# The last sum of each weight conversion job on POOL in place of DVE, in a fused attention, feed-forward and gated-attention kernel

## The chip, the cores and the metric

The kernel runs on one core of a Trainium2 chip. The metric is device time in microseconds of one launch; smaller is better. The engines are named as the profile names them: PE (TensorE), DVE (VectorE), ACT (ScalarE), POOL (GpSimd) and SP, which here only issues transfers.

## The reference

Three blocks follow one another on 4 x 576 tokens of 512 features; the conversion that the change touches prepares weights of the second.

```python
# 1: causal attention, 4 batches, 8 heads, 576 positions, head width 64, bias from cumulative sums
scores = scale * (q @ k.T); cum = cumsum(maximum(s, 0))
scores = where(causal, -1e9, scores + minimum(-(cum_i - cum_j), 0))
x = softmax(scores) @ v
# 2: mixing over positions (U 576x32, V 32x576), feed-forward (512 to 2048 to 512), residual
u = x + (x.T @ U @ V).T
x = u + maximum(u @ w_ch1, 0) @ w_ch2
# 3: four gated causal attention heads, the best two of four per token
out = sum over the chosen e of gate_e * softmax(scale * q_e @ k_e.T) @ v_e @ wo_e
```

`U`, `V`, `w_ch1` and `w_ch2` come to the kernel as bits of float64 (each value two 32-bit words) and have to be made into float32 on the chip.

## The kernel before, in words

**Split operands.** Matmuls of the feed-forward run on operands that are split in a high and a low part: ACT makes the high half as a rounded copy, DVE or POOL the low half as the difference. For weights these are `wh` (L200, ACT) and `wl` (L203, POOL), for the input `uh` (L279, ACT) and `ul` (L280; of four pieces per chunk of 288 tokens three, and in part of the kernel all but one, on POOL).

**Three parts.** Attention (to about 320 us): 32 heads, each in five row blocks, make 160 steps of one loop (`Attn.run`) and ten more to drain it. In a step PE computes a block of scores (`qk`, L364 and L365), DVE adds the mask and takes the row peak (`peak`, L375), ACT does the exponential of the step before (`exp`, L382), PE transposes what is ten steps old (L405, L408), ACT or DVE moves it out of PSUM (L78, L80), and PE multiplies it with the values (L433). When the step number divided by five leaves 1, `norm` divides the head that is done by its row sums: two small DVE operations (L387, L388) and five on POOL (L393). Then `fillers` puts background work into the step: operands of the next heads (L492, L495, L593), pieces of the weight conversion, the mixing, and the first three hidden blocks of the feed-forward.

The feed-forward part (about 320 to 675 us) runs over the other 13 hidden blocks of 128 in groups of 2, 3, 3, 3 and 2, each group over eight chunks of 288 tokens (the first group's last two chunks take the three blocks of attention along). Each step is `ffn1` (12 matmuls, L830; ACT makes `hh`, L834, and DVE its low half `hl`, L835) and, two blocks later, `ffn2` (12 matmuls, L848). At the end of a chunk's group DVE adds four accumulators to the result (L855). While a group is computed, the weights of the next are converted. In the first group the mixing of the last batch runs too (L239 to L265). The last part, the gated attention, has no conversion.

**The conversion.** `f32_stages` makes one job of a piece of weights, mostly 128x256. Its pieces: a load by SP into one of two buffers `c_raw`; a square on ACT (`p0`, L108); a masked multiply on DVE that writes `c_h` (`p1`, L111); then shift (`v0`, L115), sign (`v1`, L120), exponent (`v2`, L124), the low word scaled (`v3`, L129, again into `c_h`) and the sum (`v4`, L133), all on DVE; then `use`: for most weights `wh` on ACT (`v5`) and `wl` on POOL (`v6`). `c_a`, which the sum reads and writes, has two buffers; `c_mk`, `c_h` and `c_z` have one. In attention these three lie in unused columns of the tiles `pt`, and the profile names them so. For the first feed-forward group (`wf`) the sum writes the weights' place itself, and `v5` and `v6` do nothing.

**What sets the order.** The program is put on each engine's queue in the order in which it is written. `f32_stream` interleaves the pieces of neighbouring jobs by a table. In attention it is `STREAM`, in the feed-forward part `PLAIN`; a pair (0, 4) is `v4` of this job, (1, -1) `p1` of the next, (2, -3) the load of the one after:

```python
CONVS = ((1, 1, 1, 1, 1), (2, 2, 2, 2, 2))
PLAIN = (((0, 0),), ((0, 1),), ((0, 2), (1, -2)), ((0, 3),), ((0, 4), (2, -3)), ((1, -1),), ((0, 5),), ((0, 6),))
STREAM = (((0, 0),), ((-1, 5),), ((0, 1),), ((0, 2), (1, -2)), ((-1, 6),), ((0, 3),), ((0, 4), (2, -3)), ((1, -1),))
FAST = (40, 70)
```

In attention, from step 4, one entry of the table is put out per step, and two in steps 41 to 69, after `peak`, `exp` and `norm` of that step; the first and the third entry of the stream are put out ahead of the loop. There are 23 jobs in attention (one for U, two for V, twenty for five hidden blocks) and 12, 12, 12 and 8 in the first four feed-forward groups, where a loop puts out about five entries behind each hidden block from the fourth on (three in the fourth group), after the pieces of the input split.

Of the kernel before, what the change touches and what calls it, by code (L numbers as in the profile page):

```python
# [8 lines left out]
F32 = mybir.dt.float32  # L9
# [78 lines left out]
def f32_stages(nc, pool, width, load, m, n, name, use=None, dest=None, fixed={}):  # L88

    t_ = {}

    def tile_(tag, dt, bufs=1):
        if tag in fixed:
            t_[tag] = fixed[tag][:m, :n].bitcast(dt)
            return t_[tag]
        t_[tag] = pool.tile([P, width], dt, tag=tag, name=f"{tag}_{name}", bufs=bufs)[:m, :n]
        return t_[tag]

    def s0():
        raw = pool.tile([P, width], I64, tag="c_raw", name=f"c_raw_{name}", bufs=2)[:m, :n]
        load(raw)
        words = raw.bitcast(U32).rearrange("p (n w) -> p n w", w=2)
        t_["low"], t_["high"] = words[:, :, 0], words[:, :, 1].bitcast(F32)

    def p0():
        nc.scalar.activation(out=tile_("c_mk", F32), in_=t_["high"], func=AF.Square)  # L108

    def p1():  # L110
        nc.vector.scalar_tensor_tensor(out=tile_("c_h", F32), in0=t_["c_mk"], scalar=TINY * TINY,  # L111
                                       in1=t_["high"], op0=OP.is_ge, op1=OP.mult)

    def v0():
        nc.vector.tensor_scalar(out=tile_("c_a", U32, 2), in0=t_["c_h"].bitcast(U32), scalar1=3, scalar2=0x3FFFFFF8,  # L115
                                op0=OP.logical_shift_left, op1=OP.bitwise_and)

    def v1():

        nc.vector.scalar_tensor_tensor(out=t_["c_a"], in0=t_["c_h"].bitcast(U32), scalar=0xC0000000, in1=t_["c_a"],  # L120
                                       op0=OP.bitwise_and, op1=OP.bitwise_or)

    def v2():
        nc.vector.tensor_scalar(out=tile_("c_z", U32), in0=t_["c_a"], scalar1=0xFF800000, scalar2=None,  # L124
                                op0=OP.bitwise_and)

    def v3():

        nc.vector.scalar_tensor_tensor(out=t_["c_h"], in0=t_["low"], scalar=2.0 ** -52, in1=t_["c_z"].bitcast(F32),  # L129
                                       op0=OP.mult, op1=OP.mult)  # L130

    def v4():
        nc.vector.tensor_tensor(out=t_["c_a"].bitcast(F32) if use else dest(), in0=t_["c_h"],  # L133
                                in1=t_["c_a"].bitcast(F32), op=OP.add)

    def v5():
        if use:
            t_["u"] = use(t_["c_a"].bitcast(F32))
            next(t_["u"])

    def v6():
        if use:
            next(t_["u"], None)

    return [s0, p0, p1, (v0, v1, v2, v3, v4, v5, v6)]


# [1044 lines left out]
```

## Time and profile before

| | |
|---|---|
| time, median of 3 runs | 894.37 us (889.55 to 895.36) |
| profiled execution | 890.45 us, its span 888.6 us |
| granted TensorE clock, mean | 0.983 |
| busy: PE, DVE, ACT, POOL | 831.1, 605.1, 473.5, 308.0 us |
| sums L133 on DVE | 67 |

The span is from the first to the last instruction of the profiled execution; that execution's own time holds 1.85 us more around it. Times in the timelines count from the start of the span. In the rows, "x5" means that so many neighbouring instructions of one line are drawn together, the shape then being that of the first; a value in square brackets is the time that the engine stood idle before, and what it was released by.

### The profile page before, as it was taken

What the parts mean: (1) busy time and instruction counts of PE and PEld (TensorE: products, weight loads), DVE (VectorE), ACT (ScalarE), POOL (GpSimd) and SP (SyncE); (2) the same over time, 40 slices, a digit from 0 to 9 for tenths busy, and PEclk for the clock granted to TensorE, in tenths of its full rate; (3) what the DMA queues carried; (4) which work ended last, traced back from release to release, by engine and by line L of the source; (5) the groups of instructions that cost most, each with busy time, mean ns of one, the idle gap of its engine ahead of it and who ended that gap; (6) DMA issues with size and microseconds to landing.
All of it is one profiled execution on the core that took longest, in us unless ns stands there. A gap on an engine that the chain in (4) does not pass through costs nothing.

```text
span 888.6 us, 17507 instructions
## 1 busy us (share of the span) xinstructions
PE 831.1 (94%) x6008; PEld 745.7 (84%) x6008; DVE 605.1 (68%) x1763; ACT 473.5 (53%) x1406; POOL 308.0 (35%) x458
## 2 busy tenths in 40 slices
PE   3787988899998989999999999999999999999997
PEld 2565766688886879899999999999999999888875
DVE  7688888687577529986885788577446676646541
ACT  6577768767567353333442443333333467565673
POOL 4435454344433333322342342233233033221241
PEclk9799899899999999999999999999999999999999
DMA  8877578676662051221111121111000121211221
GB/s 217 198 200 202 148 180 214 156 184 184 182 163 69 27 192 43 49 58 27 49 49 48 48 61 48 49 44 53 1 2 1 33 49 29 63 45 35 61 68 54
DMA packets 36944, 79.65 MB, mean 90 GB/s; under 512 B 4792, under 2 KB 7992, under 8 KB 36856
## 3 DMA queue, kind: packets, MB, share of 16 engines
q1 hardware_dynamic: 36856, 78.53, 33.6%
q8 instruction: 48, 0.79, 0.4%
q14 instruction: 40, 0.33, 0.1%
HBM read 38.80 MB, written 8.40 MB: 53 GB/s over the span
## 4 chain that ended last, share of the span: by engine, by line
PE 75%; DVE 9%; DMA 5%; ACT 4%; issue 3%; POOL 2%; SPq 1%; DVEq 0%; ACTq 0%; POOLq 0%
PE hps L830 17%; PE facc L848 17%; PE pv L433 7%; PE qkp L1039 6%; PE t L405 5%; PE qk L364 4%; PE vps L976 3%; PE ops L1062 3%; PE qk L365 3%; DMA c_raw_w<-in_w_dram 3%; PE hps L296 3%; PE facc L310 3%; PE t L408 2%; ACT P L382 1%; PE mt L251 1%
## 5 line engine op out<-in xcount | busy, mean ns | idle before, releaser
L280 POOL TENSOR_TENSOR ul<-uT,uh 128x288 fp32r<-128x288 f32 x126 | 103.5, 839 | 176.7 <-ACT uh L279 164.6
L375 DVE CUSTOM_DVE_ANT_0 P<-qk,mask 64x64 f32<-64x64 f32 (+4 forms) x240 | 116.8, 488 | 61.0 <-PE qk L365 36.8
L382 ACT ACTIVATE P<-P,stat 64x64 f32<-64x64 f32 (+4 forms) x240 | 133.6, 557 | 39.7 <-DVE stat L375 37.5
L393 POOL TENSOR_SCALAR P<-P,stat 64x64 f32<-64x64 f32 (+4 forms) x160 | 101.6, 649 | 142.4 <-DVE stat L388 93.8
L364 PE MATMUL qk<-R,L 128*128 128x288 f32 (+4 forms) x288 | 98.5, 347 | 24.2 <-DVE L L577 9.8
L834 ACT ACTIVATE hh<-hps 128x288 fp32r<-128x288 f32 x110 | 44.8, 407 | 135.0 <-PE hps L830 134.6
L848 PE MATMUL facc<-hh,wh 128*128 128x288 f32 x376 | 111.2, 296 | 0.5 <-DVE aT L855 0.5
L830 PE MATMUL hps<-ul,wh 128*128 128x288 f32 x376 | 111.2, 296 | 0.0
L830 PE MATMUL hps<-uh,wl 128*128 128x288 f32 x376 | 111.1, 296 | 0.0
L830 PE MATMUL hps<-uh,wh 128*128 128x288 f32 x376 | 111.0, 295 | 0.0
L848 PE MATMUL facc<-hh,wl 128*128 128x288 f32 x376 | 110.9, 295 | 0.0
L848 PE MATMUL facc<-hl,wh 128*128 128x288 f32 x376 | 110.8, 295 | 0.0
L78 ACT ACTIVATE pt<-t 64x64 f32<-64x64 f32 (+5 forms) x304 | 90.4, 336 | 36.9 <-PE t L408 28.3
L835 DVE SCALAR_TENSOR_TENSOR hl<-hps,hh 128x288 fp32r<-128x288 f32 x110 | 50.1, 456 | 87.6 <-ACT hh L834 87.3
L405 PE MATMUL t<-ident,P 128*128 128x128 f32 x480 | 91.2, 289 | 11.0 <-issue 4.1
L393 POOL TENSOR_SCALAR P<-P,stat,pt 64x64 f32<-64x64 f32 (+4 forms) x80 | 48.2, 615 | 127.5 <-DVE stat L388 50.7
L433 PE MATMUL pv<-pt,V 128*64 128x320 f32 (+4 forms) x672 | 85.3, 378 | 7.3 <-ACT uT L78 7.3
L364 PEld LDWEIGHTS qk<-R,L 128*128 128x128 f32 x288 | 58.0, 202 | 38.9 <-issue 20.1
L365 PE MATMUL qk<-R,L 68*128 68x288 f32 (+9 forms) x288 | 90.1, 318 | 0.3
L405 PEld LDWEIGHTS t<-ident,P 128*128 128x128 f32 x480 | 60.2, 145 | 23.4 <-issue 14.0
L433 PEld LDWEIGHTS pv<-pt,V 128*64 128x64 f32 x672 | 43.7, 140 | 40.9 <-issue 12.4
L203 POOL TENSOR_TENSOR wl<-c_a_w,wh 128x256 fp32r<-128x256 f32 x56 | 43.3, 773 | 93.6 <-ACT wh L200 86.1
(177 smaller groups left out, 2211.5 us busy)
## 6 DMA issues: line engine op xcount, KB each, us to landing
c_raw_w<-in_w_dram SPq DMA_DIRECT2D x64, 256.0 KB
uT<-in_qk_dram SPq DMA_DIRECT2D x15, 576.0 KB
L<-HI SPq DMA_DIRECT2D x28, 288.0 KB
R<-HI SPq DMA_DIRECT2D x28, 288.0 KB
V<-in_v_dram SPq DMA_DIRECT2D x16, 320.0 KB
R<-uT SPq DMA_DIRECT2D x14, 288.0 KB
L<-uT SPq DMA_DIRECT2D x14, 288.0 KB
aD<-stage SPq DMA_DIRECT2D x6, 576.0 KB
```

The source lines that it names most:

```text
L78: nc.scalar.activation(out=out, in_=in_, func=AF.Copy)
L280: eng.tensor_tensor(out=l_, in0=src, in1=h_.bitcast(F32), op=OP.subtract)
L364: nc.tensor.matmul(ps[:, bk, :w], lhsT=q1[:, rows], rhs=k1[:, c0:c0 + w], start=True, stop=False)
L365: nc.tensor.matmul(ps[:, bk, :w], lhsT=q2[:, rows], rhs=k2[:, c0:c0 + w], start=False, stop=True)
L375: nc.vector.tensor_tensor_reduce(out=po, in0=view, in1=mk, scale=-1.0, scalar=3.0e38, op0=OP.add, op1=OP.min, accum_out=stat[P - M:, 0, t: ...
L382: nc.scalar.activation(out=po, in_=po, func=AF.Exp, scale=-1.0, bias=stat[P - M:, 0, t:t + 1], accum_out=stat[P - M:, 1, t:t + 1])
L393: nc.gpsimd.tensor_scalar(out=pv, in0=pv, scalar1=stat[r0:, 2, t:t + 1], scalar2=1.0 if gate is None else gate(t)[r0:], op0=OP.mult, op1=O ...
L405: nc.tensor.transpose(ps[:, P * kb:P * kb + P], Pn[:, c0:c0 + P], ident)
L433: nc.tensor.matmul(ps[64 * hh:64 * hh + 64, lo - a:e - a], lhsT=V(hh)[:, kb, :], rhs=pt[:, PST * kb + lo:PST * kb + e], start=kb == 0, sto ...
L830: nc.tensor.matmul(ps, lhsT=w[:, 0, cs], rhs=x, start=i == 0, stop=i == 11)
L848: nc.tensor.matmul(accs[c][d], lhsT=w[:, 1, cs], rhs=x, start=f == fs[0] and i == 0, stop=f == fs[-1] and i == 2)
L1039: nc.tensor.matmul(ps[:, :HALF], lhsT=wsl(w, "qk", k, col, col + P), rhs=xx[:, c0:c0 + HALF], start=i == 0, stop=i == 11)
```

## The change

The sum `v4` is issued on POOL instead of DVE. Operands, sizes and its place in the written order stay the same, and so does all else.

```diff
     def v4():
-        nc.vector.tensor_tensor(out=t_["c_a"].bitcast(F32) if use else dest(), in0=t_["c_h"],
+        nc.gpsimd.tensor_tensor(out=t_["c_a"].bitcast(F32) if use else dest(), in0=t_["c_h"],
                                 in1=t_["c_a"].bitcast(F32), op=OP.add)
```

## Rows read from the trace of the kernel before

**Rows 1.** The page of the profile: busy time of each engine; the chain by engine.

```profile
PE 831.1 (94%) x6008; PEld 745.7 (84%) x6008; DVE 605.1 (68%) x1763; ACT 473.5 (53%) x1406; POOL 308.0 (35%) x458
...
PE 75%; DVE 9%; DMA 5%; ACT 4%; issue 3%; POOL 2%; SPq 1%; DVEq 0%; ACTq 0%; POOLq 0%
```

**Rows 2.** Busy us by stretch (instructions in brackets), then PE clock, DMA share, GB/s.

```profile
60.00:100.00 40.00, 32.09 (x218) 24.41 (x215) 32.03 (x107) 30.81 (x100) 18.33 (x28) 0.92 0.80 205
...
343.00:403.00 60.00, 57.37 (x422) 56.19 (x421) 53.82 (x124) 20.09 (x55) 19.08 (x23) 1.00 0.19 49
```

**Rows 3.** What PE waited for, 345 to 403 us: total us, times, longest.

```profile
PE facc L848 <- DVE aT L855: 1.7, 2, 1.2
PE hps L830 <- DVE hl L835: 0.7, 1, 0.7
```

**Rows 4.** Timeline of PE, 357 to 371 us: start, us, operation [idle before].

```profile
357.43 0.40 PE L830 MATMUL hps<-uh,L 128*128 128x288 f32 x1 [0.69 <-DVE hl L835]
...
370.06 0.40 PE L848 MATMUL facc<-hh,L 128*128 128x288 f32 x1 [1.16 <-DVE aT L855]
```

**Rows 5.** What DVE waited for, 403 to 470 us, then 547 to 625 us.

```profile
DVE hl L835 <- ACT hh L834: 12.8, 14, 2.7
...
DVE hl L835 <- ACT hh L834: 23.9, 23, 2.7
```

**Rows 6.** Instructions of lines L133 and L203: ns minimum/median/maximum, first and last start.

```profile
L133 DVE TENSOR_TENSOR c_a_w<-c_h_w,c_a_w x44: 408/424/1060, 342.6 to 630.5; 128x256 f32<-128x256 f32 x44
L133 DVE TENSOR_TENSOR c_a_w<-pt,c_a_w x12: 415/425/548, 63.0 to 166.6; 128x256 f32<-128x256 f32 x12
...
L203 POOL TENSOR_TENSOR wl<-c_a_w,wh x56: 722/739/1230, 68.0 to 631.4; 128x256 fp32r<-128x256 f32 x56
```

**Rows 7.** Timeline of DVE in attention, around three of the jobs.

```profile
49.59 0.42 DVE L133 TENSOR_TENSOR c_a_v<-pt,c_a_v 128x288 f32<-128x288 f32 x1
...
50.94 0.56 DVE L111 SCALAR_TENSOR_TENSOR pt<-pt,c_raw_w 128x256 f32<-128x256 f32 x1
...
109.62 0.19 DVE L388 RECIPROCAL stat<-stat 128x5 f32<-128x5 f32 x1
...
112.72 0.42 DVE L111 SCALAR_TENSOR_TENSOR pt<-pt,c_raw_w 128x256 f32<-128x256 f32 x1
...
261.52 0.42 DVE L133 TENSOR_TENSOR wf<-pt,c_a_w 128x256 f32<-128x256 f32 x1
...
264.23 0.42 DVE L111 SCALAR_TENSOR_TENSOR pt<-pt,c_raw_w 128x256 f32<-128x256 f32 x1
```

**Rows 8.** Timeline of POOL around the same three jobs.

```profile
49.87 2.98 POOL L393 TENSOR_SCALAR P<-P,stat 64x64 f32<-64x64 f32 x5 [5.03 <-PE t L408]
...
110.00 4.31 POOL L393 TENSOR_SCALAR P<-P,stat 64x64 f32<-64x64 f32 x5 [2.58 <-PE mo L262]
...
261.08 4.10 POOL L393 TENSOR_SCALAR P<-P,stat 64x64 f32<-64x64 f32 x5 [5.88 <-DVE stat L388]
```

**Rows 9.** Timeline of DVE in the feed-forward part.

```profile
341.14 0.92 DVE L124 TENSOR_SCALAR c_z_w<-c_a_w 128x256 uint32<-128x256 uint32 x1
...
342.56 0.42 DVE L133 TENSOR_TENSOR c_a_w<-c_h_w,c_a_w 128x256 f32<-128x256 f32 x1
343.07 0.43 DVE L111 SCALAR_TENSOR_TENSOR c_h_w<-c_mk_w,c_raw_w 128x256 f32<-128x256 f32 x1
...
347.11 0.29 DVE L124 TENSOR_SCALAR c_z_w<-c_a_w 128x256 uint32<-128x256 uint32 x1
...
383.28 0.91 DVE L133 TENSOR_TENSOR c_a_w<-c_h_w,c_a_w 128x256 f32<-128x256 f32 x1
384.23 0.92 DVE L111 SCALAR_TENSOR_TENSOR c_h_w<-c_mk_w,c_raw_w 128x256 f32<-128x256 f32 x1
```

**Rows 10.** Timeline of POOL in the feed-forward part.

```profile
339.36 2.55 POOL L280 TENSOR_TENSOR ul<-uT,uh 128x288 fp32r<-128x288 f32 x3 [6.71 <-ACT uh L279]
...
382.16 2.70 POOL L280 TENSOR_TENSOR ul<-uT,uh 128x288 fp32r<-128x288 f32 x3 [2.71 <-ACT uh L279]
```

## The prediction

> **What bounds the kernel now.** I read the page first, for the shares of the engines and of the chain that ended last, then the busy time by stretch, then who waited for whom, and last the rows of DVE and POOL one by one around each conversion.
>
> The page says that TensorE carries 75% of the chain and DVE 9%; POOL is busy 35% of the span against DVE's 68% [rows 1]. The stretches say where it could count. In attention (up to about 320 us) no engine is full: from 60 to 100 us PE is busy 32.1 of 40 us and DVE 32.0 [rows 2], and the steps hand work round between PE, DVE, ACT and POOL. In the feed-forward part only 343 to 403 us is different: DVE is busy 53.8 of 60 us and PE has 2.6 us without work [rows 2]. All that its waits put down to an engine is DVE: 1.7 us for the sums that empty the accumulators (L855) and 0.7 us for the low halves (L835), two of them at 357 and 370 us [rows 3, 4]. In the three groups behind it PE never waits, and DVE has 12.8 us (first) to 23.9 us (last of the three) in which it waits for ACT [rows 5]. The last conversion sum starts at 630.5 us [rows 6]; behind it nothing is changed.
>
> **What the change removes.** There are 67 conversion jobs: 23 in attention, 44 in the feed-forward part. Each loses one DVE sum of about 0.42 us [rows 6]: 23 x 0.42 = 9.7 us of DVE in attention, 44 x 0.42 = 18.5 us behind it.
>
> **What it adds.** The same sum on POOL. The nearest row is L203, also a two-input fp32 operation over 128x256, at 0.74 us [rows 6]; I take that. The hand-over to POOL shows where the normalisation follows the reciprocal: that ends at 109.81 and POOL starts at 110.00, 0.19 us [rows 7, 8]. For the way back I allow 0.1 us, an estimate; 0 and 0.2 are its bounds.
>
> It also adds a wait. The next job's masked multiply (L111) overwrites c_h, of which there is one buffer, and the sum reads c_h. While both were on DVE the order cost nothing. Now L111 waits for POOL, and behind it in DVE's queue stand the row peaks (L375), the low halves and the accumulator sums, for which ACT and PE wait. In front of the sum in POOL's queue stand normalisations (five operations, 3 to 4.3 us) and u splits (L280). The raw loads on SP depend on v3, not on the sum, so they move only as DVE moves; the copy wh (L200) comes behind L111 in both orders and wl (L203) behind wh.
>
> **Attention.** A job's sum and the next L111 lie one step of the loop apart. From the written order of pieces the sum of job k falls on step 10, 18, 26, 34, then every fourth from 41 to 69, then every eighth from 77 to 157. Where the step number leaves 1 or 2 on division by five, a normalisation has just been put ahead of it in POOL's queue. That holds for nine jobs; in two of them (57 and 157) POOL is idle again or nothing follows, so seven wait. The first: the sum was ready at 49.59, POOL normalises until 52.85, so the sum ends at 53.6 and L111, which ran at 50.94, can start at 53.7: 2.75 us later [rows 7, 8]. One in the middle: 114.31 + 0.84 = 115.15 against 112.72, 2.43 us. The last: 265.18 + 0.84 = 266.02 against 264.23, 1.79 us [rows 7, 8]. The seven are 2.75, 2.23, 2.43, 1.87, 2.23, 0.99 and 1.79: 14.3 us. Each DVE sum that is gone gives 0.42 back, so DVE runs 14.3 - 2.9 = 11.4 us late in all, 1.6 us at each of seven places.
>
> How much reaches the end? At least nothing, at most 11.4. A case comes about every 40 us, and DVE idles 8 us in a stretch of that length [rows 2], five times the delay; but that idle time lies between steps that PE feeds, and PE stands as often. I take a quarter, +3.0 us, nearer the lower end.
>
> The other 16 jobs give DVE 16 x 0.42 = 6.7 us. On the chain this is worth DVE's share of 9%, 0.6 us, and at most all 6.7. Against it stands a second effect: the new POOL operation lies over DVE operations. While POOL ran three u splits (339.36 to 341.91), DVE's L124 took 0.92 us; with POOL idle it took 0.29 [rows 9, 10]. One such meeting costs more than the sum gave. I set gain and loss here to nothing, with -6.7 and 16 x 0.63 = +10.1 as ends.
>
> The Trainium skill ("SBUF — State Buffer", section "Who interferes with whom") says that a DVE instruction with two SBUF inputs, or in a two-port mode, and a GpSimd instruction that reads SBUF exclude each other for a whole instruction. The pair of L124 rows agrees. By that rule the 16 free jobs are no gain but a loss wherever such a DVE instruction follows; the end above is that case.
>
> **Feed-forward part.** About five or six pieces are issued one after another per hidden block, so L111 mostly follows the sum at once: 342.56, then 343.07 [rows 9]. With POOL free L111 would start 0.19 + 0.74 + 0.1 = 1.03 us after v3's end instead of 0.51: 0.5 us later per job. Of the twelve jobs between 343 and 404 us nine are adjacent like this. Four of them lie between 350 and 370 us, where DVE never rests more than 0.3 us and PE waits for it: 4 x 0.5, less 0.4 us of DVE idle time, is +1.6. One more, at 383.28, finds POOL in three u splits until 384.86 [rows 9, 10], so L111 moves from 384.23 to 385.7, and the accumulator sums behind it by 1.5 us; I pass on +0.9. Sum +2.5. The ends: all nine passed on and that queue, 9 x 0.5 + 1.5 = 6.0 and, for the three jobs that are not adjacent, 3 x 0.5, +7.5; or the 2.4 us of PE's waits given back, -2.4. In the other 32 jobs 0.5 us each stands against 12.8 us of idle time or more per group [rows 5]: nothing.
>
> **Sum.** +3.0 + 2.5 = +5.5 us. The profiled execution took 890.45 us (span 888.6), so 895.95; the median of the three runs is 894.37, 3.9 above it, which makes 899.9 by the median. I forecast that.
>
> **Rivals.** (a) The waits pass on in full: +11.4 in attention and +7.5 behind, 18.9 in all, 913.3. For it: DVE and PE are both at four fifths in attention, so a late peak is a late PE. Against: DVE's idle time behind each case.
> (b) The port decides: the 16 meetings at 0.63 us cost 10.1 on top of 5.5, +15.6 or 910.0. For it: L124's two rows. Against: many DVE operations beside the sums read PSUM, and one that waits on L111 meets nobody. The Trainium skill's rule ("SBUF — State Buffer", section "Who interferes with whom") leads here if it is carried through all 16.
> (c) All is hidden: 894.4. For it: PE's 75% of the chain. Against: DVE already holds PE up at 357 and 370 us [rows 4].
> (d) Faster: DVE is what attention and the stretch from 343 us wait for, and POOL delivers in time; -6.7 - 2.4 = -9.1, 885.3. It decides from the point at which L111 lies over 1.03 us behind the sum, which most attention jobs without a normalisation ahead fulfil. Against: in the crowded stretch, the one where PE demonstrably waits for DVE, L111 follows at 0.5 us.
>
> **How the numbers follow.** About 1% (8.9 us) is what a measurement of this kernel can tell from no change. The forecast has 0.42, of which 0.05 lies beyond +8.9; (a) 0.22, (b) 0.08, (c) 0.16, (d) 0.12, of which 0.10 beyond -8.9 or so. Slower: 0.05 + 0.22 + 0.08 = 0.35; faster 0.10; within 1%: 0.37 + 0.16 + 0.02 = 0.55. The range leaves out the end of (a) and most of (d): 890 to 911. The forecast's own is 896 to 905.
>
> **What would show it.** Right: L133 appears on POOL 67 times at about 0.74 us; L111 shows idle time before it put down to POOL, 1.0 to 2.8 us at seven places in attention and 0.5 us in the blocks; DVE's busy time falls by about 28 us; PE's waits for L855 and L835 between 343 and 404 us grow from 2.4 to about 5 us; attention ends 2 to 4 us later. Wrong: if attention ends earlier, (d) holds; if L111 doesn't wait but DVE's own operations beside the sums grow to 0.9 us, (b); if attention ends over 8 us later, the waits pass on whole and (a) holds.

## The result and the profile after

The changed kernel takes 897.95 us (median of 11 runs, 895.53 to 901.68) against 892.76 us of the kernel before measured beside it (median of 11, 888.9 to 895.81). The ratio is 1.0065, 95% interval 1.0045 to 1.0084: slower by 5.8 us, 4.0 to 7.5. The forecast was +5.5 us, a factor of 1.0062. The two profiled executions differ as much: spans of 894.5 and 888.6 us.

From the page of the changed kernel, the busy time of each engine and the chain by engine, to be read beside [rows 1]:

```profile
PE 833.9 (93%) x6008; PEld 745.6 (83%) x6008; DVE 577.4 (65%) x1696; ACT 473.5 (53%) x1406; POOL 354.0 (40%) x525
...
PE 74%; DVE 6%; DMA 6%; issue 5%; POOL 4%; ACT 3%; SPq 1%; POOLq 0%; ACTq 0%; DVEq 0%
```

67 instructions left DVE and 67 came to POOL. DVE is busy 27.7 us less, POOL 46.0 us more, and the kernel is slower: DVE's busy time was not what the end waited for.

The sum's line in the changed kernel (ns minimum/median/maximum, first and last start), and below it who waited for it (total us, times), to be read beside [rows 6]:

```profile
L133 POOL TENSOR_TENSOR c_a_w<-c_h_w,c_a_w x44: 727/737/743, 348.4 to 636.2; 128x256 f32<-128x256 f32 x44
L133 POOL TENSOR_TENSOR c_a_w<-pt,c_a_w x12: 727/732/742, 64.8 to 168.4; 128x256 f32<-128x256 f32 x12
...
  ACT wh L200: 64.5, 35
  DVE c_h_w L111: 27.1, 33
  DVE pt L111: 10.7, 8
```

The price of 0.74 us was right. L111 now waits for POOL 41 times: 8 times in attention (its c_h lies in a `pt` tile there), 10.7 us together, and 33 times in the feed-forward part, 27.1 us.

Where the time went is read from two fixed points, first in the kernel before, then in the changed one. The accumulator sums of the feed-forward part that write `aT` (first and last start), in the kernel before:

```profile
L855 DVE TENSOR_TENSOR aT<-facc,aT x128: 441/448/451, 335.2 to 638.0; 128x288 f32<-128x288 f32 x128
```

and in the changed kernel:

```profile
L855 DVE TENSOR_TENSOR aT<-facc,aT x128: 440/447/451, 340.9 to 644.1; 128x288 f32<-128x288 f32 x128
```

The first comes 5.7 us later and the last 6.1 us. By this pair of profiles 5.7 us were lost in attention, and 0.4 us in the stretch in which 44 of the 67 sums run.

In attention, the reciprocal of a head (L388) serves as a milestone. Three of the 32 from the timeline of DVE before (start, us):

```profile
49.49 0.19 DVE L388 RECIPROCAL stat<-stat 128x5 f32<-128x5 f32 x1
...
64.67 0.19 DVE L388 RECIPROCAL stat<-stat 128x5 f32<-128x5 f32 x1
...
299.37 0.19 DVE L388 RECIPROCAL stat<-stat 128x5 f32<-128x5 f32 x1
```

In the changed kernel these three start at 49.06, 66.88 and 305.19 us: 0.4 us early at the first, 2.2 late two heads on, 5.8 late at the end. What lies between the first two is the first of the seven places. DVE there in the changed kernel (in brackets the idle time before and what ended it):

```profile
52.91 0.43 DVE L111 SCALAR_TENSOR_TENSOR pt<-pt,c_raw_w 128x256 f32<-128x256 f32 x1 [2.65 <-POOL c_a_v L133]
...
116.12 0.43 DVE L111 SCALAR_TENSOR_TENSOR pt<-pt,c_raw_w 128x256 f32<-128x256 f32 x1 [1.35 <-POOL c_a_w L133]
...
270.09 0.43 DVE L111 SCALAR_TENSOR_TENSOR pt<-pt,c_raw_w 128x256 f32<-128x256 f32 x1 [0.63 <-POOL wf L133]
```

POOL at the first and the second of these:

```profile
49.44 2.67 POOL L393 TENSOR_SCALAR P<-P,stat 64x64 f32<-64x64 f32 x5 [5.58 <-DVE stat L388]
52.08 0.80 POOL L133 TENSOR_TENSOR c_a_v<-pt,c_a_v 128x288 f32<-128x288 f32 x1
...
111.59 3.79 POOL L393 TENSOR_SCALAR P<-P,stat 64x64 f32<-64x64 f32 x5 [3.97 <-DVE stat L388]
115.36 0.73 POOL L133 TENSOR_TENSOR c_a_w<-pt,c_a_w 128x256 f32<-128x256 f32 x1
```

and ACT behind the first:

```profile
53.92 0.67 ACT L382 ACTIVATE P<-P,stat 128x448 f32<-128x448 f32 x1 [2.60 <-DVE stat L375]
```

This is the chain of the prediction, link by link: the sum starts where the normalisation ends, L111 stands 2.65 us, the row peak behind L111 comes late, and ACT's exponential stands 2.60 us for it.

### The profile page after: what moved, and what is told of

Same layout as the page of the kernel before. It is cut to its first block, busy times and chain, and to the rows that moved or that the text cites. A ratio compares the mean times of both kernels' runs of the same rounds, so it can differ in the third digit from the quotient of the medians.

```text
span 894.5 us, 17387 instructions
## 1 busy us (share of the span) xinstructions
PE 833.9 (93%) x6008; PEld 745.6 (83%) x6008; DVE 577.4 (65%) x1696; ACT 473.5 (53%) x1406; POOL 354.0 (40%) x525
## 4 chain that ended last, share of the span: by engine, by line
PE 74%; DVE 6%; DMA 6%; issue 5%; POOL 4%; ACT 3%; SPq 1%; POOLq 0%; ACTq 0%; DVEq 0%
PE facc L848 17%; PE hps L830 17%; PE pv L433 8%; PE qkp L1039 6%; PE t L405 4%; PE vps L976 3%; PE qk L364 3%; PE ops L1062 3%; PE hps L296 3%; PE qk L365 3%; PE facc L310 2%; POOL P L393 2%; DMA c_raw_w<-in_w_dram 2%; PE t L408 2%; DMA uT<-in_qk_dram 2%
## 5 line engine op out<-in xcount | busy, mean ns | idle before, releaser
L393 POOL TENSOR_SCALAR P<-P,stat 64x64 f32<-64x64 f32 (+4 forms) x160 | 97.7, 625 | 121.8 <-DVE stat L388 86.7
L835 DVE SCALAR_TENSOR_TENSOR hl<-hps,hh 128x288 fp32r<-128x288 f32 x110 | 50.1, 456 | 85.9 <-ACT hh L834 85.8
L433 PE MATMUL pv<-pt,V 128*64 128x320 f32 (+4 forms) x672 | 88.6, 389 | 8.3 <-ACT uT L78 8.3
L405 PEld LDWEIGHTS t<-ident,P 128*128 128x128 f32 x480 | 59.7, 144 | 24.6 <-issue 11.4
L848 PEld LDWEIGHTS facc<-hh,wh 128*128 128x128 f32 x376 | 70.7, 188 | 0.9 <-issue 0.8
```

The source lines that it names most:

```text
L393: nc.gpsimd.tensor_scalar(out=pv, in0=pv, scalar1=stat[r0:, 2, t:t + 1], scalar2=1.0 if gate is None else gate(t)[r0:], op0=OP.mult, op1=O ...
L405: nc.tensor.transpose(ps[:, P * kb:P * kb + P], Pn[:, c0:c0 + P], ident)
L433: nc.tensor.matmul(ps[64 * hh:64 * hh + 64, lo - a:e - a], lhsT=V(hh)[:, kb, :], rhs=pt[:, PST * kb + lo:PST * kb + e], start=kb == 0, sto ...
L848: nc.tensor.matmul(accs[c][d], lhsT=w[:, 1, cs], rhs=x, start=f == fs[0] and i == 0, stop=f == fs[-1] and i == 2)
```

## The experiments

Theory A: the whole cost is L111's wait for POOL in attention, at the jobs that have a normalisation ahead of them. Rival B: the port; POOL's sum makes DVE's neighbours slower. A third reading is the prediction's own split, 3.0 us in attention and 2.5 behind. Every ratio is against runs of the kernel before on the same chip.

**Attention alone, feed-forward part alone.** `fixed` holds buffers in attention and is empty behind it.

```diff
-        nc.vector.tensor_tensor(out=t_["c_a"].bitcast(F32) if use else dest(), in0=t_["c_h"],
+        (nc.gpsimd if fixed else nc.vector).tensor_tensor(out=t_["c_a"].bitcast(F32) if use else dest(), in0=t_["c_h"],
```

> The sum is on POOL for the 23 jobs of attention alone, on DVE for the 44 of the feed-forward part. By the two traces the chain's steps are 5.8 us later at the end of attention and still 5.8 us later at the last accumulator sum of the group with the last conversion, so theory A (all of the cost arises in attention, through L111's wait for POOL) expects the whole of it: ratio to before 1.0065, 1.0045 to 1.0085. The split of the prediction (3.0 us in attention, 2.5 in the feed-forward part) expects 1.003, at most 1.004.

The other kernel has the two engines exchanged.

> The opposite: on DVE in attention, on POOL in the feed-forward part. Theory A expects no difference, 0.998 to 1.002, although L111 waits for POOL there some 30 times. The prediction's split expects 1.003; were the waits passed on in full, 1.008.

Measured: attention alone 1.0058 (1.0031 to 1.0084), feed-forward part alone 1.0001 (0.9984 to 1.0018). The cost is in attention. The 1.003 that the prediction's split gave for each lies just under the first interval and above the second: its term for the feed-forward part falls. The 0.4 us that the first pair of profiles showed there are not the price of the sums either. With attention alone changed, and the feed-forward part as before, the stretch between the two fixed points is as long as in the changed kernel, 303.2 us:

```profile
L855 DVE TENSOR_TENSOR aT<-facc,aT x128: 439/447/451, 344.9 to 648.1; 128x288 f32<-128x288 f32 x128
```

The waits of DVE in the kernel with the feed-forward part alone:

```profile
  POOL c_a_w L133: 27.1, 33
```

Those are all 27.1 us of the waits, and they cost nothing that can be measured.

**The seven jobs back on DVE.** `SEVEN` names the jobs that the prediction called blocked.

```diff
-        nc.gpsimd.tensor_tensor(out=t_["c_a"].bitcast(F32) if use else dest(), in0=t_["c_h"],
+        (nc.vector if fixed and name in SEVEN else nc.gpsimd).tensor_tensor(out=t_["c_a"].bitcast(F32) if use else dest(), in0=t_["c_h"],
```

> As the changed kernel, but the seven jobs of attention that were named as blocked by a normalisation keep their sum on DVE. Theory A expects most of the cost gone, since L111 waited 10.0 of its 10.7 us in attention at these seven: 0.997 to 1.003. Rival B expects 16/23 of the cost to stay: about 1.0045. A third reading, that the freed DVE time is worth nothing and any POOL work in attention delays the normalisations and u splits, expects 1.003 to 1.006.

Measured: 0.9986 (0.9970 to 1.0003). With 60 of 67 sums still on POOL the cost is gone. That speaks against B in attention, which wanted 1.0045. Between this kernel and the changed one lie 0.79%, 7.0 us (4.8 to 9.3, an estimate from the two intervals), for 10.0 us of waits less the 2.9 us that seven sums give DVE back: nearly all of the 7.1 us by the middle, two thirds at least.

**The wait alone.** Nothing is moved off DVE; POOL reads one column of c_h behind the sum. The tile `dum` is read by nobody.

```diff
     def v4():
         nc.vector.tensor_tensor(out=t_["c_a"].bitcast(F32) if use else dest(), in0=t_["c_h"],
                                 in1=t_["c_a"].bitcast(F32), op=OP.add)
+        if fixed and name in SEVEN:
+            c = t_["c_h"][:, 0:1]
+            nc.gpsimd.tensor_tensor(out=pool.tile([P, 1], F32, tag="dum", name=f"dum_{name}"), in0=c, in1=c, op=OP.add)
```

> The kernel before, with all sums on DVE, and at the seven blocked jobs one more POOL operation behind the sum that reads a single column of c_h. It moves nothing off DVE and takes POOL a small part of the 0.74 us, but L111 has to wait for it behind the normalisation. The changed kernel's L111 waited 10.0 us at the seven; without the length of the sum, some 0.7 us each, that leaves about 5 to 7 us of waits. Theory A (the waits pass on nearly in full; changed kernel against the one with seven sums on DVE: 7.0 us for 10.0 of waits less 2.9 of DVE sums) expects 4 to 7 us: ratio 1.0045 to 1.008. A quarter of them, as the prediction had it, is 1.0015 to 1.002. Rival B (the port) expects 1.000, for there is no sum on POOL.

Measured: 1.0048 (1.0028 to 1.0069), 4.3 us. DVE's waits of that kernel up to 300 us (total us, times, longest):

```profile
DVE pt L111 <- POOL dum_w L137: 6.1, 6, 1.4
...
DVE pt L111 <- POOL dum_v L137: 1.8, 1, 1.8
```

An operation of 0.19 us, seven times, slows the kernel by 4.3 us, because L111 stands 7.8 us for it (the two rows, before rounding). This is the price of the wait with nothing else changed: 4.3 / 7.8, rather over half, passes on to the end (by the interval, a third to four fifths). The same operation at the other 16 jobs:

```diff
-        if fixed and name in SEVEN:
+        if fixed and name not in SEVEN:
```

> The same one-column operation at the other 16 jobs of attention. L111 comes a step later and POOL is free, so theory A expects no wait to speak of: 0.998 to 1.002. If any handing of c_h to POOL cost time in itself, 1.003 or more.

Measured: 0.9990 (0.9969 to 1.0010). Handing c_h to POOL costs nothing where POOL is free.

**The freed DVE time.** The sum on POOL at the 16 alone:

```diff
-        nc.vector.tensor_tensor(out=t_["c_a"].bitcast(F32) if use else dest(), in0=t_["c_h"],
+        (nc.gpsimd if fixed and name not in SEVEN else nc.vector).tensor_tensor(out=t_["c_a"].bitcast(F32) if use else dest(), in0=t_["c_h"],
```

> The sum on POOL at the 16 other jobs of attention alone; the seven and the 44 of the feed-forward part on DVE. If DVE's freed time in attention (16 x 0.42 = 6.7 us) is what made the kernel with seven sums on DVE measure 0.9986, this gives the same, 0.997 to 1.000; had it been worth DVE's time in full, 0.9925. Rival B expects 1.003 to 1.005.

Measured: 0.9976 (0.9954 to 0.9999), 2.1 us faster by the middle of the interval, of 6.7 us of DVE time taken away. So it is worth something, about a third, but the interval almost reaches nothing.

**The port.** At the 16, one more full-size POOL operation that reads c_h and frees nothing:

```diff
+        if fixed and name not in SEVEN:
+            c = t_["c_h"]
+            nc.gpsimd.tensor_tensor(out=pool.tile([P, HALF], F32, tag="dum", name=f"dum_{name}")[:, :n], in0=c, in1=c, op=OP.add)
```

> The kernel before, all sums on DVE, and at the 16 jobs of attention without a normalisation ahead one more POOL operation of full size that reads c_h (256 columns, some 0.74 us) into a tile that nobody reads. It frees nothing on DVE; L111 should mostly find it done. It prices what POOL's reading costs DVE's neighbours: rival B expects 16 x 0.63 = 10.1 us at most, 1.005 to 1.011; theory A 0.999 to 1.002.

Measured: 0.9982 (0.9959 to 1.0005), with 14 of the 16 extra operations at 0.70 us each (median). L111 waits for none of them. Rival B's 10 us are not there, although the meetings took place: the extra operation lay over ten of the sums on DVE; four of those took 0.51 to 0.84 us in place of 0.42, and at five others the extra operation itself took 0.85 us or more in place of 0.61. The Trainium skill's rule ("SBUF — State Buffer", section "Who interferes with whom") agrees with the single meeting, as the L124 rows of [rows 9, 10] show it; in attention sixteen chances of one add up to nothing measurable.

**c_h set free.** v3 writes its product over c_z, the sum reads c_z, and L111 has no more business with POOL.

```diff
     def v3():
 
-        nc.vector.scalar_tensor_tensor(out=t_["c_h"], in0=t_["low"], scalar=2.0 ** -52, in1=t_["c_z"].bitcast(F32),
+        nc.vector.scalar_tensor_tensor(out=t_["c_z"].bitcast(F32), in0=t_["low"], scalar=2.0 ** -52, in1=t_["c_z"].bitcast(F32),
...
     def v4():
-        nc.gpsimd.tensor_tensor(out=t_["c_a"].bitcast(F32) if use else dest(), in0=t_["c_h"],
+        nc.gpsimd.tensor_tensor(out=t_["c_a"].bitcast(F32) if use else dest(), in0=t_["c_z"].bitcast(F32),
```

> All 67 sums on POOL, but v3 writes its product over c_z in place of c_h, and the sum reads c_z. L111 then has nothing of POOL to wait for; the next writer of c_z, v2 of the next job, comes three to five pieces later. Same operations, sizes and engines as the changed kernel. Theory A (the wait on c_h is the cost) expects the cost gone: 0.994 to 1.001, L111 without idle time put down to POOL. Rival B (the port: POOL's sum beside DVE's two-input operations costs the time) expects the time to stay, 1.005 to 1.010, for there are now more such meetings, not fewer.

Measured: 1.0013 (0.9997 to 1.0028), L111 without any wait for POOL. Most of the cost is gone, but not all that theory A had promised (at most 1.001). The control has the same two lines with the sum on DVE:

> The kernel before with v3 written over c_z and the sum reading c_z, all on DVE. It moves nothing between engines: 0.998 to 1.002. If it is slower by 0.1% or more, the remainder of 1.0013 of the kernel with the sum on POOL and c_h free is the new place of v3's product and not POOL.

Measured: 0.9969 (0.9945 to 0.9993), faster, where nothing was expected. Both were repeated beside one another:

> The same kernel as the one with v3 written over c_z and all on DVE, which measured 0.9969 where no change was expected. If that was no accident of one set of runs, 0.995 to 0.998 again; if it was, 0.999 to 1.002.

Measured: 0.9979 (0.9958 to 0.9999).

> The same kernel as the one with all sums on POOL and c_h free, 1.0013 beside other runs of before, now beside the kernel with c_z alone. If a sum on POOL costs something even when L111 does not wait for it (rival B, or sums that come late for wh behind a normalisation), it stays 0.2 to 0.5% above that kernel; theory A alone expects the two within 0.15%.

Measured: 1.0026 (1.0003 to 1.0050). With L111's wait out of the way, moving the sum still costs about 0.4%, 4 us. The accumulator sums say where. With c_z and the sum on DVE:

```profile
L855 DVE TENSOR_TENSOR aT<-facc,aT x128: 440/447/451, 335.8 to 637.0; 128x288 f32<-128x288 f32 x128
```

With c_z and the sum on POOL:

```profile
L855 DVE TENSOR_TENSOR aT<-facc,aT x128: 440/447/451, 338.4 to 643.5; 128x288 f32<-128x288 f32 x128
```

From first to last that is 301.2 us against 305.1 us, and the first pair of profiles had 301.2 and 305.0. Here the feed-forward part does pay, 3.9 us (2.3 us against the 302.8 us of the kernel before). PE's waits of 325 to 430 us, with the sum on DVE, go from

```profile
PE facc L848 <- DVE aT L855: 0.7, 2, 0.5
PE hps L830 <- DVE hl L835: 0.6, 3, 0.3
```

to, with the sum on POOL,

```profile
PE facc L848 <- DVE aT L855: 2.4, 2, 1.8
PE hps L830 <- DVE hl L835: 2.0, 3, 1.1
```

which is 3.1 of the 3.9. The timeline of the latter kernel, all engines, shows one such wait:

```profile
359.31 0.42 DVE L111 SCALAR_TENSOR_TENSOR c_h_w<-c_mk_w,c_raw_w 128x256 f32<-128x256 f32 x1
...
359.47 0.86 POOL L133 TENSOR_TENSOR c_a_w<-c_z_w,c_a_w 128x256 f32<-128x256 f32 x1 [3.42 <-DVE c_z_w L129]
...
360.36 0.42 ACT L200 ACTIVATE wh<-c_a_w 128x256 fp32r<-128x256 f32 x1 [4.51 <-POOL c_a_w L133]
360.68 0.39 ACT L834 ACTIVATE hh<-hps 128x288 fp32r<-128x288 f32 x1
...
361.10 0.46 DVE L835 SCALAR_TENSOR_TENSOR hl<-hps,hh 128x288 fp32r<-128x288 f32 x1 [1.38 <-ACT hh L834]
...
361.62 0.40 PE L830 MATMUL hps<-uh,L 128*128 128x288 f32 x1 [1.14 <-DVE hl L835]
```

The wait has changed its queue. ACT's copy wh needs the sum, stands for POOL, and the high half hh of the next block stands behind it in ACT's queue; then DVE's low half and PE wait in turn. In the changed kernel ACT stands at wh as well, over the whole kernel 64.5 us for POOL where it was 54.4 us for DVE before, and the feed-forward part loses nothing that can be measured. Why the same delay of wh is free with c_h and costs 3.9 us with c_z, where DVE doesn't stand but goes on past L111, was not tried apart. The meetings of DVE and POOL may have a part in it: L111 now runs beside the sum, as in the rows above, and from 340 to 640 us L111 takes 586 ns in the mean (501 with the sum on DVE) and the sum 806 ns (736 in the changed kernel). On DVE's side it is little where PE waits: from 336 to 410 us the five other DVE operations of the twelve jobs (L111 to L129) take 30.0 us together against 29.0 with the sum on DVE. The longer sum, for which wh waits, comes on top.

**Both edits that measured faster.**

> v3 over c_z and the sum on POOL at the 16 jobs of attention without a normalisation ahead, DVE for the rest: the two edits that each measured faster, 0.9969 and 0.9976. If both are real and add up, 0.993 to 0.996; if they are one effect, or none, 0.997 to 1.000.

v3 over c_z as above, and the engine chosen as in the kernel with the 16. Measured: 0.9968 (0.9948 to 0.9989), median 887.56 us against 891.99. It beats both kernels of this case; that it is more than c_z alone (0.9969 and 0.9979) can't be said.

## Why the prediction was right

The time (+5.5 us forecast, +5.8 measured) and the mechanism in attention are confirmed: L111's wait for the sum behind a normalisation, at the seven jobs worked out from the written order. That the sum came out so close is luck. The prediction put 3.0 us in attention and 2.5 behind it; the kernels that change one part alone show 5.2 us (2.8 to 7.5) and 0.1 us (-1.4 to 1.6). Four terms were off and made up for one another.

- **The seven waits, 14.3 us.** They came to 2.65, 1.35, 1.35, 1.73, 1.35, 0.89 and 0.63 us, 10.0 us. Of the 4.3 us that are missing, 3.5 are the normalisations, which the working took at their old length: in the changed kernel all seven are shorter (2.67 us against 2.98 at the first place, 3.79 against 4.31 at the second shown). Another 0.7 us is DVE, which came to L111 later after their start at four of the seven and earlier at three. There was an eighth wait, of 0.77 us, at a job that the prediction had set aside because POOL would be idle again (step 57): a normalisation, and behind it a low half `wl`, held POOL until L111 was due, and L111 stood for the sum's own length.
- **"I take a quarter".** More passes on: 4.3 us for 7.8 in the kernel that has only the wait, and 7.0 for 7.1 between the changed kernel and the one with the seven back on DVE. Their intervals meet between two thirds and four fifths. DVE's 8 us of idle time in 40 did not cover the waits. That much of this idle time is itself a wait for PE and ACT, which a late peak delays in turn, is a reading of the waits (ACT stood 2.60 us behind the first of them) and was not tried apart.
- **The 16 other jobs, "gain and loss to nothing".** Gain was 2.1 us by the middle of the interval (0.1 to 4.1), and a loss by the port could not be measured.
- **The feed-forward part, +2.5 us.** It cost 0.1 us by the ratio, and the 0.4 us in the profile are there without the sums too. The hand-overs were taken too long, at 0.19 and 0.1 us. The timeline of the changed kernel has a job in the crowded stretch:

```profile
361.06 0.43 DVE L129 SCALAR_TENSOR_TENSOR c_h_w<-c_raw_w,c_z_w 128x256 f32<-128x256 uint32 x1
...
361.56 0.74 POOL L133 TENSOR_TENSOR c_a_w<-c_h_w,c_a_w 128x256 f32<-128x256 f32 x1 [3.28 <-DVE c_h_w L129]
...
362.34 0.43 DVE L111 SCALAR_TENSOR_TENSOR c_h_w<-c_mk_w,c_raw_w 128x256 f32<-128x256 f32 x1 [0.86 <-POOL c_a_w L133]
```

  POOL starts 0.07 us after v3's end and L111 0.04 us after the sum: 0.85 us where 1.03 was allowed, so 0.3 us later per job and not 0.5. PE's waits for L855 and L835 from 345 to 410 us are these in the changed kernel, against [rows 3] (345 to 403 us):

```profile
PE facc L848 <- DVE aT L855: 1.5, 3, 0.6
PE hps L830 <- DVE hl L835: 1.3, 2, 0.7
```

  That is 2.8 us and not 5, against 2.4 in [rows 3], or 2.6 with the 0.26 us at 344.28 us, whose counterpart lies in the later window. The job that finds POOL in three u splits, for which the prediction added 0.9 us, waits longest:

```profile
387.42 2.52 POOL L280 TENSOR_TENSOR ul<-uT,uh 128x288 fp32r<-128x288 f32 x3 [2.40 <-ACT uh L279]
389.91 0.73 POOL L133 TENSOR_TENSOR c_a_w<-c_h_w,c_a_w 128x256 f32<-128x256 f32 x1
...
390.67 0.43 DVE L111 SCALAR_TENSOR_TENSOR c_h_w<-c_mk_w,c_raw_w 128x256 f32<-128x256 f32 x1 [2.16 <-POOL c_a_w L133]
```

  In the kernel before, the sum and L111 themselves took 0.91 and 0.92 us there, beside the u splits [rows 9, 10]. In the changed kernel L111 takes 0.43 us, and it ends 5.95 us later than before, no more than the 5.7 to 6.1 us by which this whole part is late; PE stood 0.4 us for L855 behind it. The step that failed is the one that let five jobs act on PE at 0.5 us and more each; DVE stood 27.1 us in place of 18.5 us of sums, and its idle time held nearly all of the difference.

With the measured terms, in the prediction's own form: 10.7 us of waits at eight places, less 0.42 us for each sum that is gone there, are 7.3 us. At seven tenths, where the two measurements of the share meet, they are 5.1; less some 2 us of freed time this is 3 us in attention, inside the interval of the kernel with attention alone (2.8 to 7.5 us) but near its lower end. So the sizes are not fully told, and the share that passes on least of all.

Of the signs that the prediction named, the waits at the seven places came (0.6 to 2.65 us for 1.0 to 2.8), and DVE's busy time fell by 27.7 us for 28. Attention ended 5.7 us later for 2 to 4, and PE's waits in the crowded stretch hardly grew.

Of the rivals, (a) had the right cause and in attention twice the price, 11.4 us for 5.2; behind it, 7.5 us for nothing that can be measured. (b), the port, fell in attention by the extra POOL operations. (c), all hidden, holds for the feed-forward part, where the prediction gave it too little. (d), faster, may have its grain of truth in the 16 jobs; it needs the seven left on DVE.

## What to carry to other kernels

An operation that moves to an idle engine takes its buffer with it: an order that one queue had kept for nothing becomes a wait of the next writer, and that wait lasts as long as whatever stands ahead in the new queue. Before moving one, list who overwrites its inputs and what the new engine has queued at that point; here the seven of 23 jobs that stood behind a normalisation carried the cost, and leaving them where they were removed it. Taking one wait away is not enough either: the next reader of the result, here ACT's copy, may hold up its own queue in its stead.

## What had not been expected

Writing v3's product over c_z, with all on DVE, made the kernel faster twice, 0.9969 and 0.9979, though it moves no work. In the feed-forward part the stretch from the first to the last accumulator sum falls from 302.8 to 301.2 us. DVE's idle time ahead of L111 from 340 to 640 us shows part of it. Before, and then with c_z:

```profile
L111 DVE SCALAR_TENSOR_TENSOR c_h_w<-c_mk_w,c_raw_w 128x256 f32<-128x256 f32 x43 | 22.2, 517 | 2.3 <-ACT c_mk_w L108 0.5
```

```profile
L111 DVE SCALAR_TENSOR_TENSOR c_h_w<-c_mk_w,c_raw_w 128x256 f32<-128x256 f32 x43 | 21.6, 501 | 0.5 <-ACT c_mk_w L108 0.5
```

The 2.3 us before it become 0.5. While c_h was shared, L111 stood a moment for the sum ahead of it on its own engine: 32 of these jobs have the two side by side, and L111 started 0.03 to 0.09 us after the end of the sum, with c_z 0.08 us ahead of it. In the one stretch where PE waits for DVE that is worth having. That this is the whole reason was not shown.

Profiles of attention differ by as much as the effects looked for. With attention as before and only the feed-forward part changed, the first accumulator sum came at 337.1 us against 335.2; with attention as in the changed kernel and the rest as before, at 344.9 against 340.9. So the ratios over many runs, and not single pairs of traces, decide between the parts here. All traces together agree with them: in the three kernels whose L111 stands for POOL at the seven jobs the first accumulator sum comes at 340.9 to 344.9 us, in the other eleven traces at 332.5 to 338.4.
